# Even chunks, freely issued row-tile blocks and strip maxima on GpSimd in an attention-plus-gate kernel

## The chip, the cores and the metric

The kernel runs on one core of one Trainium2 chip. The metric is device time in microseconds, taken over several executions; one further execution was profiled. A core has TensorE (PE in the profile, its weight loads PEld), VectorE (DVE), ScalarE (ACT), GpSimd (POOL), SyncE (SP), which issues nearly all transfers here, and 16 DMA engines. Each engine runs its own instructions in order and waits on semaphores for the others.

## The reference

```python
# x: [4, 12800, 128], inducing: [32, 128]
def mab(q, kv):
    s = scale * (q @ kv.transpose(0, 2, 1))
    s = s - s.max(-1, keepdims=True)
    a = np.exp(s)
    a /= a.sum(-1, keepdims=True) + 1e-09
    return a @ kv
h = mab(I, x)              # 32 inducing points attend to all tokens of a batch
x = mab(x, h)              # every token attends to the 32 results
...
for k in range(5):         # causal filter of 5 taps along the tokens, per channel
    gate_pre += conv_w[k] * xp[:, k:k + S, :]
gate = 1.0 / (1.0 + np.exp(-gate_pre))
return (gate * (x @ w_val)) @ w_out
```

## The kernel before, in words

Each batch of 12,800 tokens is cut into four strips of 3,200, and the strips into chunks (`SIZES`): in batch 0 eight chunks of 128 to 512 columns, in batches 1 to 3 seven, 480, five times 512, and 160. A chunk always means those columns of all four strips; the strips lie on the four groups of 32 partitions. Two copies of x come from memory: channel-major `xt` (11 buffers) and token-major `xk` (4 buffers); in batch 0 most of `xk` is made on PE from `xt` instead (`make_xk`, letter x).

The first attention goes chunk by chunk. `s1` makes scores with the inducing points (four products side by side, one per strip) and DVE takes them out of PSUM with their maximum. `gmax` combines the maxima of a group of chunks (`GROUPS`) over tokens and strips: a PE product with the identity turns the column of 128 into a row (L420), DVE takes the maximum over strips (L426), small PE products spread it over the partitions again (L434), and DVE scales it (L441). These two halves are the letters gm and gn. `e1` takes exp on ACT and transposes 32x32 blocks on DVE; `h` multiplies with `xk` (L474) and accumulates. `prep` (u) merges the groups and normalises, `prep1` (t) turns the 32x128 result on PE (L532), `prep2` and `prep3` (w, W) scale h by the taps and by w_val and turn that into row-tile weights in two fp16 parts, and `prep_out` (po, pp) finds one scale for the output weights, again over PE (L621, L636).

The second attention, `s2`, makes scores with h (L679), and passes through DVE, POOL, ACT, DVE, POOL, DVE, ACT and POOL to the normalised weights P in two fp16 parts, P1 and P2.

Then come the row-tile blocks (`rblock`). For each chunk and strip, 15 gate units (five taps in three fp16 combinations, L751) and 3 value units (L760) are products with only 32 rows, so the four strips run side by side on the four row tiles of the array. Each chunk has two half blocks. In a half block two strips end their gate units, and the two others do the value units of a chunk and begin the gate units of the next; `SPLIT = 6` gate units stand in the block that begins a gate, nine in the block that ends it, and units are issued row by row over the four strips. After it ACT takes tanh of the gate (L816), DVE multiplies it with the value (L827), ACT and POOL split the product into two fp16 halves (L841, L847), PE multiplies by the output weights (`outp`, L866 to L868), and DVE or ACT evacuates (`evac`, L879 or L881, chosen by `OUTV`), and SP stores.

PE's order is written out by hand: `START` lists everything ahead of the first block, `LEAD` how many half blocks ahead each `s2` stands, `FILL` where the next batch's steps stand between blocks; the two `outp` of a half block follow the next half block. All other engines' orders, SP's included, come from a planner (`Plan.order`): a list schedule with fixed costs, lags and `URGE` offsets, whose due times come from PE's order. The planner makes a fixed program; nothing is decided at run time. Each tile kind has a fixed number of buffers (`BUFS`), and a new user waits for the readers of the buffer that it takes over. Loads also wait for the block `AHEAD` blocks earlier. [...]

Of the kernel before, what the change touches and what calls it, by code (L numbers as in the profile page):

```python
# [29 lines left out]
SIZES = [[128, 256, 512, 512, 512, 512, 512, 256]] + [[480, 512, 512, 512, 512, 512, 160]] * 3  # L30
# [10 lines left out]
SWITCH = 0.09  # L41
# [7 lines left out]
class Plan:  # L49
# [77 lines left out]
    def lay(self, deps, succ, topo, nominal):  # L127
# [8 lines left out]
        free, bus = {}, 1.25  # L136
# [47 lines left out]
def tile_kernel(ctx: ExitStack, tc: tile.TileContext, xt, xk, indT_in, w64, out):  # L184
# [24 lines left out]
    def f_const():  # L209
        warm = const.tile([P, 1], F32, name="warm")  # L210
        V.memset(warm, 0.0)
# [5 lines left out]
        ones = const.tile([P, P], F32, name="ones")  # L217
        V.memset(ones, 1.0)
# [4 lines left out]
        c_.update(ident=ident, identf=identf, ones=ones, pick=pick)  # L223
# [98 lines left out]
    def load_xt(b, c, u=1):  # L322
# [83 lines left out]
    def gmax(b, g):  # L406

        cs = GROUPS[b][g]
        ng = len(GROUPS[b])
# [8 lines left out]
        def f1():
            t = pt(key)
            T.matmul(t[:1, :P], st[m1], c_["identf"], start=True, stop=True)  # L420
# [3 lines left out]
        def f2():
            m = sb(pw, mr, [1, M])
            V.tensor_reduce(m, st[key][:1, :P].rearrange("p (r j) -> p j r", r=R), AX.X, ALU.max)  # L426

        i2 = op("DVE", 0.27, f2, [i1], 0.0, [mr], [key])

        def second():  # L430
            def f4():
                t = pt(key2)
                for r in range(R):
                    T.matmul(t[32 * r:32 * r + 32, :1], st[mr], c_["ones"][:1, :1], start=True, stop=True)  # L434

            i4 = PE(0.17, f4, [i2], [key2], [mr], "strips", 0.12)

            def f5():
                if g == 0:
                    sb(pb, ("ng", b), [P, ng], F32, [P, NCK])  # L440
                V.tensor_scalar(st["ng", b][:, g:g + 1], st[key2][:, :1], -SCALE, None, ALU.mult)  # L441

            ix["ng", b, g] = op("DVE", 0.15, f5, [i4], 0.0, [("ng", b)] * (g == 0), [key2] + [("ng", b)] * (g > 0))

        return second
# [44 lines left out]
    def prep(b):  # L490
# [37 lines left out]
    def prep1(b):  # L528
        key = ("a", "ht", b)

        def f5():
            T.transpose(pt(key)[:, :M], st["hn", b], c_["identf"][:M, :M])  # L532

        i = PE(0.17, f5, [ix["hn", b]], [key], [("hn", b)], lag=0.15)
        ix["hT", b] = op("DVE", 0.18, lambda: V.tensor_copy(sb(pb, ("hT", b), [P, M]), st[key][:, :M]), [i], 0.0,
                         [("hT", b)], [key])

    def prep2(b):
# [77 lines left out]
    def prep_out(b):  # L616

        vmx, wk = ("vmx", b), ("a", "wk", b)

        def f0():  # L620
            T.matmul(pt(wk)[:1, :P], st["q", b], c_["identf"], start=True, stop=True)  # L621

        i0 = PE(0.25, f0, [ix["gsc", b], i_const], [wk], [("q", b)], lag=0.15)

        def f1():
            m = sb(pw, ("qm", b), [1, 1])
            V.tensor_reduce(m, st[wk][:1, :P], AX.X, ALU.max)
            V.tensor_scalar(m, m, TINY, 1.0 / SO, ALU.max, ALU.mult)

        i1 = op("DVE", 0.44, f1, [i0], 0.0, [("qm", b)], [wk])  # L630

        def second():
            key = ("a", "wk2", b)

            def f2():
                T.matmul(pt(key)[:, :1], c_["ones"][:1, :], st["qm", b], start=True, stop=True)  # L636

            i2 = PE(0.2, f2, [i1], [key], [("qm", b)], lag=0.15)

            def f3():  # L640
                V.tensor_scalar(sb(pb, ("osc", b), [P, 1]), st[key][:, :1], 0.5 / SP, None, ALU.mult)
                u = pw.tile([P, 1], F32, name="u")
                V.reciprocal(u, st[key][:, :1])
                V.tensor_scalar(u, u, st[vmx], None, ALU.mult)
                st["u", b] = u

            i = op("DVE", 0.5, f3, [i2], 0.0, [("osc", b)], [key, vmx])
            i = op("ACT", 0.3, lambda: S.activation(sb(pw, ("wof", b), [P, P]), c_["wout"], AF.Copy, scale=st["u", b]), [i],
                   0.0, [("wof", b)])
            i = op("ACT", 0.3, lambda: S.copy(sb(pb, ("wo", b), [P, 2, P], F16)[:, 0], st["wof", b]), [i], 0.0,  # L650
                   [("wo", b)], [("wof", b)])

            def f4():
                G.tensor_tensor(st["wo", b][:, 1], st["wof", b], st["wo", b][:, 0], ALU.subtract)

            ix["wo", b] = op("POOL", 0.42, f4, [i], 0.0, [], [("wof", b), ("wo", b)])

        return second

# [4 lines left out]
    def s2(b, c):  # L664
# [98 lines left out]
    SPLIT = 6  # L763
    seqs = [(b, c) for b in range(B) for c in range(len(SIZES[b]))]

    def rblock(k, half):
# [7 lines left out]
        deps, use, newv, newg = [], [], [], []  # L774
        if cur:
            for r in ends:
                work[r] += [(gate_mm, *cur, r, u) for u in range(SPLIT, len(taps))]
                use.append((f"g{r}", *cur))
        for r in other:
            if val:  # L780
                newv.append(("a", "v", *val, r))
            if nxt:
                newg.append((f"g{r}", *nxt))
            work[r] += [(val_mm, *val, r, u) for u in range(3)] if val else [None] * 3
            work[r] += [(gate_mm, *nxt, r, u) for u in range(SPLIT)] if nxt else []
        for bc in (cur, val, nxt):
            if bc:
                deps += [ix[("P", *bc)], ix["W", bc[0], 1]]
                use += [k for k in (("W", bc[0]),) if k not in use]
        depth = max(len(w) for w in work.values())  # L790

        def part(us, new):
            todo = [[work[r][u] for r in range(R) if u < len(work[r]) and work[r][u]] for u in us]

            def f():
                for row in todo:
                    for fn, *a in row:
                        fn(*a)

            return PE(sum(COST["unit"] * max(SIZES[w[1]][w[2]] for w in row) for row in todo if row) + 0.02,  # L800
                      f, deps, new, use, "rows", 0.34)
# [70 lines left out]
    def evac(b, c, r, i):  # L872
# [57 lines left out]
    def po(b):  # L930
        sec[b, "o"] = prep_out(b)

    def pp(b):
# [139 lines left out]
```

## Time and profile before

| | |
|---|---|
| median of 3 runs | 305.16 us (304.87 to 305.18) |
| profiled execution, its own time | 303.38 us |
| span of the profiled execution, first to last instruction | 301.5 us |
| mean granted clock of PE | 0.984 |
| busy, PE / DVE / ACT / POOL | 286.3 / 236.5 / 216.1 / 204.1 us |
| memory read and written | 48.69 and 26.21 MB |

The page gives busy time per engine, the span in slices, the chain of work that ended last, and groups of instructions by source line with their mean duration. In a timeline row the first number is the start in us, the second the length of the merged piece, and a bracket at the end gives the engine's idle time before it and what ended that. In a row of stretches come the stretch, its length, then busy time and count of PE, PEld, DVE, ACT and POOL, then PE's granted clock (1.00 is full), the DMA engines' mean busy share and GB/s. In a row of groups the numbers are busy us and mean ns, then idle before. A row of waits says who waited for whom: us in total, times, longest.

### The profile page before, as it was taken

To read this page: it belongs to the slowest core of one execution; us is meant where nothing else is said; L and a number is where in the kernel's file an instruction comes from. 1 tells how busy PE (TensorE), PEld (TensorE's weight loads), DVE (VectorE), ACT (ScalarE), POOL (GpSimd) and SP (SyncE) were. 2 spreads that over 40 slices of the span, in tenths; PEclk is the share of its full clock that TensorE was granted. 3 is DMA by queue.
4 is the path that set the end of the run, shared out by engine and by line. 5 is a ranking of instruction groups with operands and counts; after the bars stand their busy time and mean duration, and the time that the engine had idled before them with its cause. 6 is when DMAs were issued, how large, how long until landed. Compare 5 with 4: busy or idle time off the path is not lost.

```text
span 301.5 us, 10231 instructions
## 1 busy us (share of the span) xinstructions
PE 286.3 (95%) x4100; PEld 138.5 (46%) x4100; DVE 236.5 (78%) x597; ACT 216.1 (72%) x421; POOL 204.1 (68%) x229
## 2 busy tenths in 40 slices
PE   7998889999998999999999979999999999999994
PEld 2666435554443346545435324635453444434342
DVE  1568899996695998889668867899788996977562
ACT  2665247587566985887677664789777789889893
POOL 1000457888374798659754494797877999999761
PEclk9999799999999999999999988999999999999998
DMA  7999999698898738979883596922323233244434
GB/s 291 427 407 421 420 417 367 244 404 304 307 357 329 262 127 288 353 273 333 315 296 137 174 361 241 327 95 111 143 104 142 106 133 113 80 157 162 168 141 183
DMA packets 24526, 75.55 MB, mean 251 GB/s; under 512 B 2848, under 2 KB 7456, under 8 KB 19360
## 3 DMA queue, kind: packets, MB, share of 16 engines
q1 hardware_dynamic: 24336, 74.90, 66.0%
q8 instruction: 32, 0.52, 0.7%
q14 instruction: 14, 0.11, 0.1%
q10 hardware_dynamic: 144, 0.02, 0.0%
HBM read 48.69 MB, written 26.21 MB: 248 GB/s over the span
## 4 chain that ended last, share of the span: by engine, by line
PE 69%; DMA 17%; DVE 7%; ACT 3%; issue 2%; SPq 1%; POOL 0%; POOLq 0%; ACTq 0%; DVEq 0%
PE g L751 23%; DMA out_dram<-os 8%; PE a L679 7%; PE a L866 7%; PE a L474 6%; DMA xt<-in_xt_dram 6%; PE a L760 6%; PE a L868 5%; PE a L867 5%; PE a L394 5%; DMA xk<-in_xk_dram 3%; ACT os L881 1%; DVE os L879 1%; PE a L600 1%; DVE tg L827 1%
## 5 line engine op out<-in xcount | busy, mean ns | idle before, releaser
L847 POOL TENSOR_TENSOR gl<-tg,gh 128x512 f16<-128x512 f32 (+4 forms) x112 | 115.4, 1045 | 34.9 <-ACT gh L841 34.2
L751 PE MATMUL g<-P,W 32*128 32x512 f16 (+4 forms) x1740 | 115.0, 345 | 0.2 <-ACT tg L816 0.2
L841 ACT CAST gh<-tg 128x512 f16<-128x512 f32 (+4 forms) x112 | 62.2, 569 | 23.0 <-DVE tg L827 22.5
L827 DVE SCALAR_TENSOR_TENSOR tg<-tg,a 128x512 f32<-128x512 f32 (+4 forms) x116 | 65.7, 604 | 11.8 <-PE a L760 9.5
L751 PEld LDWEIGHTS <-W 32*128 32x128 f16 x1740 | 54.1, 92 | 43.4 <-issue 14.0
L816 ACT ACTIVATE tg<-g,gsc 128x512 f32<-128x512 f32 (+4 forms) x116 | 67.6, 624 | 2.7 <-PE g L751 2.1
L881 ACT ACTIVATE os<-a,osc 128x512 f32<-128x512 f32 (+4 forms) x58 | 36.0, 631 | 15.7 <-PE a L868 9.7
L879 DVE TENSOR_SCALAR os<-a,osc 128x512 f32<-128x512 f32 (+4 forms) x58 | 37.4, 661 | 10.4 <-PE a L868 6.0
L760 PE MATMUL a<-P,W 32*128 32x512 f16 (+4 forms) x348 | 43.7, 348 | 0.7 <-DVE ss L402 0.5
L866 PE MATMUL a<-gh,wo 128*128 128x512 f16 (+4 forms) x112 | 40.0, 359 | 1.4 <-ACT os L881 1.4
L868 PE MATMUL a<-gl,wo 128*128 128x512 f16 (+4 forms) x112 | 39.4, 354 | 0.1
L867 PE MATMUL a<-gh,wo 128*128 128x512 f16 (+4 forms) x112 | 39.4, 354 | 0.0
L737 POOL TENSOR_TENSOR P<-pt,P 128x512 f16<-128x512 f32 (+2 forms) x29 | 30.0, 1037 | 6.4 <-ACT P L730 6.2
L719 POOL TENSOR_TENSOR e<-e,z 128x512 f32<-128x512 f32 (+2 forms) x29 | 27.2, 939 | 8.5 <-DVE z L713 3.3
L394 PE MATMUL a<-xt,indT 128*32 128x512 f32 (+4 forms) x232 | 29.1, 566 | 3.7 <-DMA xt<-in_xt_dram 3.0
L696 POOL TENSOR_TENSOR e<-e,m 128x512 f32<-128x512 f32 (+2 forms) x29 | 27.2, 938 | 5.6 <-DVE m L690 5.1
L474 PE MATMUL a<-xk,et 128*32 128x129 f32 x800 | 28.5, 281 | 1.9 <-DMA xk<-in_xk_dram 0.8
L679 PE MATMUL a<-xt,hT 128*32 128x512 f32 (+2 forms) x232 | 27.4, 556 | 0.0
L474 PEld LDWEIGHTS a<-xk,et 128*32 128x32 f32 x800 | 23.1, 112 | 9.0 <-issue 3.3
L402 DVE TENSOR_SCALAR_CACHE_REDUCE ss<-a 128x512 f32<-128x512 f32 (+4 forms) x29 | 17.5, 606 | 10.9 <-PE a L394 10.2
L702 ACT ACTIVATE e<-e 128x512 f32<-128x512 f32 (+2 forms) x29 | 16.7, 578 | 8.7 <-POOL e L696 8.6
L866 PEld LDWEIGHTS <-wo 128*128 128x128 f16 x112 | 10.8, 97 | 26.4 <-issue 17.6
(104 smaller groups left out, 304.3 us busy)
## 6 DMA issues: line engine op xcount, KB each, us to landing
xt<-in_xt_dram SPq DMA_DIRECT2D x23, 1024.0 KB, 8.7
out_dram<-os SPq DMA_DIRECT2D x80, 256.0 KB, 2.5
xk<-in_xk_dram SPq DMA_DIRECT2D x17, 1032.0 KB, 8.0
xk<-in_xk_dram SPq DMA_DIRECT2D x3, 967.5 KB, 8.8
out_dram<-os SPq DMA_DIRECT2D x12, 240.0 KB, 2.1
xt<-in_xt_dram SPq DMA_DIRECT2D x4, 320.0 KB, 5.5
xt<-in_xt_dram SPq DMA_DIRECT2D x2, 512.0 KB, 8.5
out_dram<-os SPq DMA_DIRECT2D x8, 128.0 KB, 7.5
```

Of the source, the lines that this page charges most:

```text
L394: T.matmul(s[32 * r:32 * r + 32, :n], c_["indT"], x[:, o:o + n // 32, r, :], start=True, stop=True)
L474: T.matmul(t[32 * s:32 * s + 32, :P + 1], e[:, 32 * i:32 * i + 32], x[:, m + i, :], start=i < R, stop=i >= nb - R)
L679: T.matmul(s[32 * r:32 * r + 32, :n], st["hT", b], x[:, m:m + nb, r, :], start=True, stop=True)
L751: T.matmul(st[f"g{r}", b, c][:, :n], st["W", b][q, w, k, :], st[("P1", "P2")[e]][q, o:o + n], start=u == 0, stop=u == len(taps) - 1)
L760: T.matmul(st["a", "v", b, c, r][:, :n], st["W", b][q, w, TAPS, :], st[("P1", "P2")[e]][q, o:o + n], start=u == 0, stop=u == 2)
L816: S.activation(t[:, :n], st[f"g{r}", b, c][:, :n], AF.Tanh, scale=st["gsc", b])
L827: V.scalar_tensor_tensor(t[:, :n], t[:, :n], 1.0, st["a", "v", b, c, r][:, :n], ALU.add, ALU.mult)
L841: S.copy(t, st[tg][:, :n])
L847: G.tensor_tensor(sb(pw, g2, [P, 512], F16)[:, :n], st[tg][:, :n], st[g1][:, :n], ALU.subtract)
L866: T.matmul(t, w[:, 0], st[g1][:, :n], start=True, stop=False)
L867: T.matmul(t, w[:, 1], st[g1][:, :n], start=False, stop=False)
L868: T.matmul(t, w[:, 0], st[g2][:, :n], start=False, stop=True)
```

## The change

- Sizes: batches 1 and 2 get chunks of 448 and 480 columns; batches 0 and 3 keep theirs.
- The number of gate units on each side is chosen per half block by a small dynamic programme over the chunk sizes (`begun`), 6 and 9 in most of batches 1 and 2, up to 8 and down to 1 elsewhere; and within a block each strip's units are put out in the order in which the strips' time is used up, without rows.
- Group maxima over strips and the output scale go from PE to POOL: two maxima of partition halves, then four scalings, one per strip. `gn` and `pp` go away. In batches 1 to 3 h is turned by four 32x32 transposes on DVE.
- In the half blocks listed in `HOLD` the waiting outputs stay until a later block.
- `START`, `FILL`, `LEAD`, `URGE`, `XEV`, `OUTV`, `AHEAD`, batch 0's groups and some of the planner's costs are new; `START` has six groups of filler products (z) on zeros, 11 in all.

```diff
-SIZES = [[128, 256, 512, 512, 512, 512, 512, 256]] + [[480, 512, 512, 512, 512, 512, 160]] * 3
+SIZES = [[128, 256, 512, 512, 512, 512, 512, 256]] + [[448, 448, 448, 448, 448, 480, 480]] * 2 + [[480, 512, 512, 512, 512, 512, 160]]
...
+def begun(n, units, even):
+    last = len(n) - 1
+    ways = {a: (a * n[0] + even * n[0] * (a - 6) ** 2, [a]) for a in range(units + 1)}
+    for k in range(len(n)):
...
+                first = max((units - a) * n[k], (3 * n[k - 1] if k else 0) + b * n[k]) + even * n[k] * (b - 6) ** 2
+                for d in range(units + 1) if k < last else (0,):
+                    second = max((units - b) * n[k], 3 * n[k] + (d * n[k + 1] if k < last else 0))
...
 def gmax(b, g):
-        i1 = PE(0.25, f1, [i0, i_const], [key], [m1], lag=0.2)
...
+            over_strips(st[m1])
+            for r in range(R):
+                G.tensor_scalar(st["ng", b][32 * r:32 * r + 32, g:g + 1], st[m1][:M, 2:], -SCALE, None, ALU.mult)
+        ix["ng", b, g] = op("POOL", 1.3, f1, [i], 0.0, [("ng", b)] * (g == 0), [m1] + [("ng", b)] * (g > 0))
+    def over_strips(m):
+        G.tensor_scalar(m[:2 * M, 1:2], m[:2 * M, :1], m[2 * M:, :1], None, ALU.max)
+        G.tensor_scalar(m[:M, 2:], m[:M, 1:2], m[M:2 * M, 1:2], None, ALU.max)
...
 def prep1(b):
+        def f6():
+            t = sb(pb, ("hT", b), [P, M])
+            for r in range(R):
+                V.transpose(t[32 * r:32 * r + 32], st["hn", b][:, 32 * r:32 * r + 32])
...
 def prep_out(b):
+            V.transpose(t, st["q", b].broadcast_to([P, M]))
+            V.tensor_reduce(sb(pw, qm, [P, 3])[:, :1], t, AX.X, ALU.max)
...
+            over_strips(st[qm])
+            for r in range(R):
+                G.tensor_scalar(u[32 * r:32 * r + 32], st[qm][:M, 2:], TINY, 1.0 / SO, ALU.max, ALU.mult)
+            G.tensor_scalar(sb(pb, ("osc", b), [P, 1]), u, 0.5 / SP, None, ALU.mult)
...
 def rblock(k, half):
+            while any(work.values()) and (whole or any(w and w[0][0] is val_mm for w in work.values())):
+                r = min((r for r in range(R) if work[r]), key=lambda r: (spent[r], r))
+                fn, b, c, r, u = work[r].pop(0)
+                todo.append((fn, b, c, r, u))
+                spent[r] += COST["unit"] * SIZES[b][c]
...
-            for o in late:
-                outp(*o)
-            late = [(*seqs[q], r) for r in rs] if 0 <= q < len(seqs) else []
+            if 2 * k + half not in HOLD:
+                for o in late:
+                    outp(*o)
+                late = []
+            late += [(*seqs[q], r) for r in rs] if 0 <= q < len(seqs) else []
...
-OUTV = [(2, 3), (0, 2), (0, 1), (0, 2)]
-AHEAD = 18
+OUTV = [(0,), (2,), (2, 3), (2,)]
+AHEAD = 11
+TURNED = (0,)
+EVEN = 0.02
+HOLD = (0, 5, 7, 9, 13, 16, 19, 24, 28, 31, 38, 40, 43)
```

In batch 0 the new START makes `xk` of chunks 0, 2, 3, 1, 5 and 6 on PE (before: 0, 2, 1, 3, 5 and 7) and loads 4 and 7 (before: 4 and 6). Ahead of the first block it also holds `s1` of chunk 3 and the products `h` of chunks 0 and 2 of batch 1; before, those came later, and `s1` of chunks 0, 1 and 2 were there in both.

More of the change, by code (lines that the diff above doesn't have):

```diff
@@ L1 @@
+import functools
 import itertools
@@ L40 @@
 OWN = 0.035
-SWITCH = 0.09
+SWITCH = dict(full=0.09, rows=0.095, strips=0.117)
 COST = dict(
@@ L88, in order @@
             deps[b].append(a)
-            ops[a]["turn"] = SWITCH * (ops[a]["kind"] != ops[b]["kind"])
+            ops[a]["turn"] = SWITCH[ops[a]["kind"]] * (ops[a]["kind"] != ops[b]["kind"])
         succ = [[] for _ in range(n)]
@@ L135, in lay @@
                 late[i] = min(late[i], late[s] - ops[i]["dur"] - ops[i]["lag"])
-        free, bus = {}, 1.25
+        free, bus = {}, 1.45
         end = [0.0] * n
@@ L175, in lay @@
         return seq, at, end
+@functools.lru_cache(None)
+def begun(n, units, even):
+    last = len(n) - 1
+    ways = {a: (a * n[0] + even * n[0] * (a - 6) ** 2, [a]) for a in range(units + 1)}
+    for k in range(len(n)):
+        more = {}
+        for a, (c, way) in ways.items():
+            for b in range(units + 1):
+                first = max((units - a) * n[k], (3 * n[k - 1] if k else 0) + b * n[k]) + even * n[k] * (b - 6) ** 2
+                for d in range(units + 1) if k < last else (0,):
+                    second = max((units - b) * n[k], 3 * n[k] + (d * n[k + 1] if k < last else 0))
+                    v = c + first + second + (even * n[k] * (d - 6) ** 2 if k < last else 0)
+                    if d not in more or v < more[d][0]:
+                        more[d] = v, way + [b, d]
+        ways = more
+    return min(ways.values())[1]
 def cost(kind, n):
@@ L216, in f_const @@
         make_identity(nc, identf)
-        ones = const.tile([P, P], F32, name="ones")
-        V.memset(ones, 1.0)
         pick = const.tile([P, M], F32, name="pick")
@@ L222, in f_const @@
             st[k] = const.tile([P, XW], F16, name=k)
-        c_.update(ident=ident, identf=identf, ones=ones, pick=pick)
+        c_.update(ident=ident, identf=identf, pick=pick)
     def f_ind():
@@ L332, in f @@
             nc.sync.dma_start(st[key][:, first:first + n // 32].rearrange("p i r q -> p (i r q)"), xt[b, :, o:o + R * n])
-        ix["xt", b, c, u] = sp(n * 2048 / BW + 1.9 * ((b, c) == (0, 2)), f, [key] * own, [key] * (not own))
+        ix["xt", b, c, u] = sp(n * 2048 / BW + 1.2 * ((b, c) == (0, 2) and ("xt", 0, 1, 1) in ix), f, [key] * own, [key] * (not own))
     def load_xk(b, c):
@@ L409, in gmax @@
         ng = len(GROUPS[b])
-        key, key2 = ("a", "gm", b, g), ("a", "gn", b, g)
-        m1, mr = ("m1", b, g), ("mr", b, g)
+        m1 = ("m1", b, g)
         def f0():
-            V.tensor_reduce(sb(pw, m1, [P, 1]), st["mx", b][:, cs[0]:cs[-1] + 1], AX.X, ALU.max)
-        i0 = op("DVE", 0.15, f0, [ix["ss", b, c] for c in cs], 0.0, [m1], [("mx", b)])
+            V.tensor_reduce(sb(pw, m1, [P, 3])[:, :1], st["mx", b][:, cs[0]:cs[-1] + 1], AX.X, ALU.max)
+        i = op("DVE", 0.15, f0, [ix["ss", b, c] for c in cs], 0.0, [m1], [("mx", b)])
         def f1():
-            t = pt(key)
-            T.matmul(t[:1, :P], st[m1], c_["identf"], start=True, stop=True)
-        i1 = PE(0.25, f1, [i0, i_const], [key], [m1], lag=0.2)
[L424 to L445, printed above, removed]
+            if g == 0:
+                sb(pb, ("ng", b), [P, ng], F32, [P, NCK])
+            over_strips(st[m1])
[5 more added lines that the diff above has]
+        G.tensor_scalar(m[:M, 2:], m[:M, 1:2], m[M:2 * M, 1:2], None, ALU.max)
     def e1(b, g, c):
@@ L501, in prep @@
         i0 = op("DVE", 0.15, f0, [ix["ng", b, g] for g in gs] + [i_const], 0.0, [f_], [("ng", b)])
-        i0 = op("ACT", 0.2, lambda: S.activation(st[f_], st["ng", b], AF.Exp, bias=st["mt", b], scale=-1.0), [i0], 0.0, [],
+        i0 = op("ACT", 0.29, lambda: S.activation(st[f_], st["ng", b], AF.Exp, bias=st["mt", b], scale=-1.0), [i0], 0.0, [],
                 [f_, ("ng", b)])
@@ L508, in f1 @@
                 S.activation(sb(pw, Ds[g], [P, M]), c_["pick"], AF.Copy, scale=st[f_][:, g:g + 1])
-        i0 = op("ACT", 0.13 + 0.16 * len(gs), f1, [i0], 0.0, Ds, [f_])
+        i0 = op("ACT", 0.1 + 0.215 * len(gs), f1, [i0], 0.0, Ds, [f_])
         Hs = [("H", b, g) for g in gs]
@@ L529, in prep1, with f5 @@
         key = ("a", "ht", b)
[L531 to L536, printed above, removed]
+        if b in TURNED:
+            def f5():
+                T.transpose(pt(key)[:, :M], st["hn", b], c_["identf"][:M, :M])
+            i = PE(0.17, f5, [ix["hn", b]], [key], [("hn", b)], lag=0.15)
+            ix["hT", b] = op("DVE", 0.18, lambda: V.tensor_copy(sb(pb, ("hT", b), [P, M]), st[key][:, :M]), [i], 0.0,
+                             [("hT", b)], [key])
+            return
+        def f6():
+            t = sb(pb, ("hT", b), [P, M])
+            for r in range(R):
+                V.transpose(t[32 * r:32 * r + 32], st["hn", b][:, 32 * r:32 * r + 32])
+        ix["hT", b] = op("DVE", 0.84, f6, [ix["hn", b]], 0.0, [("hT", b)], [("hn", b)])
     def prep2(b):
@@ L561, in g1 @@
                             st[cg][:, :, None].broadcast_to([P, TAPS, M]), ALU.mult)
-        ig = op("POOL", 0.65, g1, [i], 0.0, [wf, cg], [("hT", b)])
+        ig = op("POOL", 0.81, g1, [i], 0.0, [wf, cg], [("hT", b)])
         ih = op("ACT", 0.325, lambda: S.copy(sb(pw, w2, [P, 2, TAPS + 1, M], F16)[:, 0, :TAPS], st[wf]), [ig], 0.0,
@@ L616, in prep_out @@
     def prep_out(b):
-        vmx, wk = ("vmx", b), ("a", "wk", b)
+        vmx, tq, qm = ("vmx", b), ("tq", b), ("qm", b)
         def f0():
-            T.matmul(pt(wk)[:1, :P], st["q", b], c_["identf"], start=True, stop=True)
-        i0 = PE(0.25, f0, [ix["gsc", b], i_const], [wk], [("q", b)], lag=0.15)
+            t = sb(pw, tq, [P, M])
+            V.transpose(t, st["q", b].broadcast_to([P, M]))
+            V.tensor_reduce(sb(pw, qm, [P, 3])[:, :1], t, AX.X, ALU.max)
+        i = op("DVE", 0.4, f0, [ix["gsc", b]], 0.0, [tq, qm], [("q", b)])
@@ L625, in f1 @@
         def f1():
[L626 to L656, printed above, removed]
@@ L658, in prep_out, with f2 @@
-        return second
+            u = st["u", b] = pw.tile([P, 1], F32, name="u")
+            over_strips(st[qm])
+            for r in range(R):
+                G.tensor_scalar(u[32 * r:32 * r + 32], st[qm][:M, 2:], TINY, 1.0 / SO, ALU.max, ALU.mult)
+            G.tensor_scalar(sb(pb, ("osc", b), [P, 1]), u, 0.5 / SP, None, ALU.mult)
+        i = op("POOL", 1.5, f1, [i], 0.0, [("osc", b)], [qm])
+        def f2():
+            u = st["u", b]
+            V.reciprocal(u, u)
+            V.tensor_scalar(u, u, st[vmx], None, ALU.mult)
@@ new lines, in prep_out, with f4 @@
+        i = op("DVE", 0.38, f2, [i], 0.0, [], [vmx])
+        i = op("ACT", 0.35, lambda: S.activation(sb(pw, ("wof", b), [P, P]), c_["wout"], AF.Copy, scale=st["u", b]), [i],
+               0.0, [("wof", b)])
+        i = op("ACT", 0.32, lambda: S.copy(sb(pb, ("wo", b), [P, 2, P], F16)[:, 0], st["wof", b]), [i], 0.0,
+               [("wo", b)], [("wof", b)])
+        def f4():
+            G.tensor_tensor(st["wo", b][:, 1], st["wof", b], st["wo", b][:, 0], ALU.subtract)
+        ix["wo", b] = op("POOL", 0.42, f4, [i], 0.0, [], [("wof", b), ("wo", b)])
@@ L713, in sm @@
                 V.memset(z[:M, 0, :1], 0.0)
-        i = op("DVE", cost("dve", n) + 0.52, sm, [i], 0.0, [zk], [ek])
+        i = op("DVE", cost("dve", n) + 0.55, sm, [i], 0.0, [zk], [ek])
         def nm():
@@ L761, in val_mm @@
                  start=u == 0, stop=u == 2)
-    SPLIT = 6
     seqs = [(b, c) for b in range(B) for c in range(len(SIZES[b]))]
+    split = begun(tuple(SIZES[b][c] for b, c in seqs), len(taps), EVEN)
     def rblock(k, half):
@@ L773, in rblock @@
         work = {r: [] for r in range(R)}
-        deps, use, newv, newg = [], [], [], []
         if cur:
             for r in ends:
-                work[r] += [(gate_mm, *cur, r, u) for u in range(SPLIT, len(taps))]
-                use.append((f"g{r}", *cur))
+                work[r] += [(gate_mm, *cur, r, u) for u in range(split[2 * k + half], len(taps))]
         for r in other:
[L780 to L785, printed above, removed]
+            work[r] += [(val_mm, *val, r, u) for u in range(3)] if val else []
@@ L786, in rblock @@
+            work[r] += [(gate_mm, *nxt, r, u) for u in range(split[2 * k + half + 1])] if nxt else []
+        deps, held = [], []
         for bc in (cur, val, nxt):
-            if bc:
+            if bc and any(w[1:3] == bc for l in work.values() for w in l):
                 deps += [ix[("P", *bc)], ix["W", bc[0], 1]]
[L789 to L793, printed above, removed]
-            def f():
[L796 to L801, printed above, removed]
@@ L803, in rblock, with part @@
-        i0 = part(range(3), newv)
-        i = part(range(3, depth), newg)
+                held += [k for k in (("W", bc[0]),) if k not in held]
+        spent = {r: 0.0 for r in range(R)}
+        def part(whole):
+            todo, new, use, before = [], [], list(held), max(spent.values())
+            while any(work.values()) and (whole or any(w and w[0][0] is val_mm for w in work.values())):
[3 more added lines that the diff above has]
+                spent[r] += COST["unit"] * SIZES[b][c]
+                key = ("a", "v", b, c, r) if fn is val_mm else (f"g{r}", b, c)
+                if u == 0:
+                    new.append(key)
+                elif key not in new and key not in use:
+                    use.append(key)
+            def f():
+                for fn, *a in todo:
+                    fn(*a)
+            return PE(max(spent.values()) - before + 0.02, f, deps, new, use, "rows", 0.34)
@@ L805, in rblock @@
+        i0 = part(False) if val else None
+        i = part(True)
         blocks.append(i)
@@ L883, in evac @@
         v = r in OUTV[b]
-        j = op("DVE" if v else "ACT", cost("psum", n) if v else cost("act", n) + 0.06, ev, [i], 0.0, [os], [key, ("osc", b)])
+        j = op("DVE" if v else "ACT", cost("psum", n) + 0.07 if v else cost("act", n) + 0.06, ev, [i], 0.0, [os], [key, ("osc", b)])
         def store():
@@ L940, in xs @@
         make_xk(b, c, XEV[c])
-    do = dict(s1=S1, z=idle, gm=gm, gn=gn, h=hh, x=xs, u=prep, t=prep1, w=prep2, k=load_xk,
-              W=prep3, po=po, pp=pp, s2=s2, l=lambda b, c: ("xt", b, c, 1) in ix or load_xt(b, c))
+    do = dict(s1=S1, z=idle, gm=gmax, h=hh, x=xs, u=prep, t=prep1, w=prep2, k=load_xk,
+              W=prep3, po=prep_out, s2=s2, l=lambda b, c: ("xt", b, c, 1) in ix or load_xt(b, c))
     for b, f, *a in START:
@@ L1023 @@
 WARM = 8
-LEAD = [[10.5, 0, 11.5, 6.5, 2.5, 13, 6.5, 6.5], [2, 2, 3, 9.5, 3.5, 4, 7.5], [1.5, 3, 2, 6, 3.5, 6, 5.5], [3.5, 4, 6, 6.5, 8, 6, 5]]
-AHEAD = 18
+LEAD = [[-9.5, 13, 0.5, 8, 4.5, 13, 4, 6], [2, 4.5, 4.5, 3, 5, 5.5, 14], [1.5, 2, 3.5, 7.5, 4.5, 3.5, 11.5], [3, 7.5, 2.5, 7.5, 11, 8.5, 2.5]]
+AHEAD = 11
 AGAIN = [(), (), (), ()]
-BUFS = dict(xt=11, wf=2, cg=2, hn=2, wof=1, xk=4, ss=4, et=3, e=3, pt=2, tg=5, gh=4, gl=4, q=2, qm=2, osc=2, os=4, H=4, mx=2, ng=2, m1=2, mr=2, f=2, D=6, hT=2,
+BUFS = dict(xt=11, wf=2, cg=2, hn=2, wof=1, xk=4, ss=4, et=3, e=3, pt=2, tg=5, gh=4, gl=4, q=2, qm=2, tq=2, osc=2, os=4, H=4, mx=2, ng=2, m1=2, f=2, D=6, hT=2,
             gmx=2, vmx=2, gsc=2, wo=2, w2=2, W=2, m2=3, z=3, a=4, g0=1, g1=1, g2=1, g3=1)
```

17 lines of the change are left out of this document (4 added, 13 removed), and 37 rows, old and new, of tables (FILL, START).

## The prediction

> **What bounds the kernel now.** I read the page's engine rows, slices and chain first, then a table of stretches, then the tensor engine's own waits.
>
> ```profile
> span 301.5 us, 10231 instructions
> PE 286.3 (95%) x4100; PEld 138.5 (46%) x4100; DVE 236.5 (78%) x597; ACT 216.1 (72%) x421; POOL 204.1 (68%) x229
> PE 69%; DMA 17%; DVE 7%; ACT 3%; issue 2%; SPq 1%; POOL 0%; POOLq 0%; ACTq 0%; DVEq 0%
> ...
> 30.00:40.00 10.00, 8.91 (x124) 4.60 (x127) 8.79 (x39) 2.21 (x5) 3.81 (x8) 0.83 1.01 421
> ...
> 90.00:100.00 10.00, 8.55 (x104) 3.38 (x103) 6.64 (x15) 6.28 (x11) 4.53 (x5) 1.00 0.88 330
> ...
> 160.00:180.00 20.00, 17.65 (x278) 7.50 (x272) 16.52 (x36) 15.40 (x27) 13.05 (x14) 0.98 0.63 221
> ...
> 240.00:260.00 20.00, 19.82 (x286) 9.09 (x282) 16.83 (x39) 18.09 (x39) 19.59 (x22) 1.00 0.29 106
> 260.00:280.00 20.00, 20.00 (x246) 7.96 (x236) 15.87 (x31) 18.64 (x34) 19.50 (x20) 1.00 0.41 156
> ```
>
> PE is busy 95% of the span and carries 69% of the chain; no other engine passes 78%. After about 60 us nearly every stretch has PE at 20.0 of 20 us, so the time there is the sum of what PE is given to do, plus a few waits. Before that, the opening mixes loads and latency. Two cautions: POOL is at 98% from 240 to 280 us (19.59 and 19.50 of 20) and ACT at 90 to 93%, so helpers have little room late.
>
> ```profile
> PE a L866 <- ACT os L881: 1.4, 1, 1.4
> ...
> 179.37 1.94 PE L394 MATMUL a<-xt,indT 128*32 128x512 f32 x8 [2.00 <-DMA xt<-in_xt_dram]
> 33.00:34.00 1.00, 1.00 (x33) 0.79 (x32) 0.96 (x4) 0.25 (x1) 0.67 (x2) 0.50 1.05 429
> 180.00:181.00 1.00, 1.00 (x8) 0.25 (x4) 0.00 (x0) 0.00 (x0) 1.00 (x1) 0.50 0.98 355
> ```
>
> Later waits are few: 2.0 us for one x tile at 179 us, 1.4 us for one evacuation, some tenths elsewhere. Twice the granted clock is halved (0.50 in the last two rows). The first time it makes the 0.83 of the stretch 30 to 40 us: 0.17 of 10 us, 1.7 us lost; I take the same for the second.
>
> **The change, part by part.** The sum is made against the profiled span of 301.5 us. That execution took 303.38 us, 1.88 us more than its span; the median of the runs shown, 305.16 us, is 0.6% above it. I add my difference to the median.
>
> *Row-tile blocks.* A block runs two lists of 32-row matmuls, two tiles each, concurrently, and lasts as long as the longer list. Before, gate units were split 9 and 6 everywhere and the four tiles went row by row, so where a 512-column chunk is followed by one of 160 the lists are 9x512 = 4608 against 3x512+6x160 = 2496 columns, and one pair of tiles idles. Summing the longest list over all 60 blocks from SIZES gives 243,648 columns before. With the new chunks, the chosen splits and each tile going on freely, the same sum is 235,104; perfectly even would be 230,400. The difference is 8,544 columns. The price:
>
> ```profile
> 269.67 0.39 PE L751 MATMUL g<-P,W 32*128 32x512 f16 x2
> ...
> 271.73 0.39 PE L866 MATMUL a<-gh,wo 128*128 128x512 f16 x1
> ...
> 169.81 1.06 PE L679 MATMUL a<-xt,hT 128*32 128x512 f32 x8
> 170.81 0.39 PE L760 MATMUL a<-P,W 32*128 32x512 f16 x2
> ...
> 87.45 1.06 PE L679 MATMUL a<-xt,hT 128*32 128x512 f32 x8
> 88.33 1.04 PE L394 MATMUL a<-xt,indT 128*32 128x512 f32 x8
> ```
>
> A score product takes 1.00 us start to start when a block follows (169.81 to 170.81) and 0.88 when another score product does (87.45 to 88.33): a change between full, strip and row shapes costs 0.12 us. A block of nine 512-column steps takes 271.73-269.67 = 2.06 us, less 0.12 is 1.94, or 0.215 us for 512 columns. So 8,544 columns are **-3.6 us**, nearly all after 60 us, where PE has no other bound.
>
> *Matmuls that leave PE.* The group maximum (L420, then L434), the output scale (L621, L636) and the turned h (L532) leave PE, the last in three batches of four.
>
> ```profile
> 195.80 1.06 PE L679 MATMUL a<-xt,hT 128*32 128x512 f32 x8
> 196.68 0.38 PE L420 MATMUL a<-identf,m 128*1 128x128 f32 x2
> 196.99 0.39 PE L751 MATMUL g<-P,W 32*128 32x512 f16 x2
> ...
> 200.04 0.24 PE L434 MATMUL a<-ones,mr 1*32 1x1 f32 x8
> 200.21 0.38 PE L866 MATMUL a<-gh,wo 128*128 128x480 f16 x1
> ...
> 185.84 0.38 PE L621 MATMUL a<-identf,q 128*1 128x128 f32 x2
> 186.15 0.39 PE L866 MATMUL a<-gh,wo 128*128 128x512 f16 x1
> 191.88 0.38 PE L636 MATMUL a<-qm,ones 1*128 1x1 f32 x2
> 192.12 0.45 PE L760 MATMUL a<-P,W 32*128 32x480 f16 x2
> ...
> 218.22 0.19 PE L532 MATMUL a<-identf,hn 32*128 32x32 f32 x1
> 218.34 0.39 PE L866 MATMUL a<-gh,wo 128*128 128x512 f16 x1
> ```
>
> Start to start they cost 0.31 (less 0.12 for the shape change that stays: 0.19), 0.17, 0.31, 0.24 and 0.12 us. Six group maxima and three of each other kind lie in batches 1 to 3: 6x0.36 + 3x0.55 + 3x0.12 = 4.2 us. Batch 0's share, 3x0.36 + 0.55 = 1.6 us, lies in the opening, where PE partly waits anyway; I take half. **-5.0 us** (bounds -4.2 and -5.8).
>
> *Shape changes.* Writing out PE's order from START, FILL, LEAD and HOLD, without those matmuls, gives 146 changes of shape from block (2,1) on before and 134 after: where HOLD lets outputs wait, four follow in one go. 12 x 0.12 = **-1.4 us**. In the opening it is 31 and 29, which I count as nothing: PE waits there in any case, and would cost 0.2 us without that cover.
>
> *What PE gets in addition.* Chunk 6 instead of chunk 7 is transposed on PE, 76 transposes for 68.
>
> ```profile
> 20.07 1.97 PE L370 MATMUL g<-identf,xt 128*128 128x128 f32 x16
> 21.97 0.27 PE L420 MATMUL a<-identf,m 128*1 128x128 f32 x1
> 26.25 2.70 PE L474 MATMUL a<-xk,et 128*32 128x129 f32 x77 [0.81 <-DMA xk<-in_xk_dram]
> L895 PE MATMUL a<-zero 128*128 128x512 f16 x8 | 3.6, 631 | 1.2 <-DVE warm L211 1.2
> ```
>
> Sixteen take 1.90 us, so eight more are 0.95, and a fourth group in batch 0 about 0.1: **+1.05 us**. Eleven filler matmuls (z) stand in the opening, at most 3.6/8 = 0.45 us each, 5.0 us together, at the cold rate, and half of that at full clock, 2.5. Most stand where PE waited (the 0.81 us above is one such wait; the stretch 30 to 40 us has 1.09 us idle). I take **+0.5**, bounds 0 and +2.5. They fill the sparse time ahead of the first half-clock stretch; avoiding it would bring 1.7 us, not avoiding it nothing: **-0.8**. [...]
>
> *Loads.* Chunk 4's token-major tile was the fifth in a pool of four, so it waited for a product and PE then for it, 0.81 us; now it is the fourth: **-0.8**. x tiles still reuse 11 buffers. Adding up PE's order at the prices above, the wait at 179 us came where the product that frees the buffer stands 6.6 us of work ahead of its next user; the closest such pairs after 60 us are then 7.7 and 8.5 us apart.
>
> ```profile
> DMA to landing us min/median/max: 5.4/6.8/8.2
> ```
>
> With landings of 5.4 to 8.2 us there, that wait may shrink but isn't gone. AHEAD 11 for 18 lets loads start later, but eleven blocks are at least 11 x 2.06 = 23 us, and a landing is 8.2: nothing.
>
> *What the other engines get.* Rows that set the prices:
>
> ```profile
> L559 POOL TENSOR_SCALAR cg<-w,gs 128x5 f32<-128x5 f32 x4 | 1.1, 273 | 9.6 <-DVE vmx L571 8.5 <-DVE gs L553 1.0
> L881 ACT ACTIVATE os<-a,osc 128x512 f32<-128x512 f32 (+4 forms) x58 | 36.0, 631 | 15.7 <-PE a L868 9.7
> L881 ACT ACTIVATE os<-a,osc 128x160 f32<-128x160 f32 x6 | 2.4, 398 | 1.8 <-DMA out_dram<-os 1.1 <-PE a L858 0.6
> ```
>
> POOL gets 10 group maxima of six small operations and 4 output scales of seven, 88 at no more than the 0.27 us of a small operation: up to 24 us, from 204 to at most 228 of about 292 us. OUTV moves 22 evacuations from DVE to ACT, 22 x 0.63 = 14 us: ACT 230. DVE falls by about as much, less the 32x32 transposes it gains. None becomes the busiest; I cost this at nothing because PE's fixed order covers it. Without that cover each group maximum could hold back a product and everything behind it. The end does change: three of the last four 160-column evacuations are now on ACT, one more at 0.4 us, of which **+0.3** shows.
>
> *The remaining waits* after 60 us (1.45, 2.35 and 0.18 us idle in three stretches of the table, 4.0 together, and 1.7 us of half clock) I leave as they are: a new order removes some and makes others. Bounds: -6 if all go; +8 if they more than double, from the 98% POOL and the 93% ACT above.
>
> Sum: -3.6 -5.0 -1.4 +1.05 +0.5 -0.8 -0.8 +0.3 = -9.75 us: span 291.8, the median 295.4 us.
>
> **The rivals.** *Savings become waits.* PE asks for each result 3% sooner from helpers that are 90 to 98% busy late; for it speak the 98% POOL, against it that PE waits for none of them from 260 to 280 us (20.0 of 20). At 4 to 9 us given back: 299 to 304.5 us.
>
> *The waits go as well.* The second half clock (1.7), the 2.0 and the 1.4 us and most of the tenths go, 5 to 7 us more: 288.5 to 290.5 us.
>
> *Slower, by the group maximum on GpSimd.* Six dependent small operations stand in POOL's queue behind operations of over 1 us, then exp, transpose and the product that PE has at a fixed place. Chain: 0.68 (maximum per chunk) + 6x0.27 + 0.72 (exp) + 0.70 (transpose) = 3.7 us after the last score product.
>
> ```profile
> L402 DVE TENSOR_SCALAR_CACHE_REDUCE ss<-a 128x512 f32<-128x512 f32 x20 | 13.5, 680 | 5.6 <-PE a L394 5.2
> L453 ACT ACTIVATE ss<-ss,ng 128x512 f32<-128x512 f32 x20 | 13.7, 716 | 3.1 <-DVE ng L441 3.1
> L458 DVE STREAM_TRANSPOSE et<-ss 128x512 f32<-128x512 f32 x20 | 13.8, 697 | 0.8 <-ACT ss L453 0.8
> ```
>
> The shortest room, counted the same way, is some 4.5 us (batch 1, first group) and 6 to 7 in batch 3. It decides against the change from 1 us lost at each of ten groups, which takes queues of 3 us or more: 306 to 309 us. [...]
>
> *The change doesn't do what it says:* if the tiles don't run on freely, the first term shrinks, to about -2.5 us (the new chunks alone, counted in the old manner): 296.5, inside the forecast's range.
>
> **How the numbers follow.** Forecast (291 to 298.5 us) 0.57; savings become waits 0.20; waits go as well 0.13; slower 0.07; within 0.2%, about what a measurement can tell (304.5 to 305.8), 0.03. So 295.4 us; the range, leaving out some of the two outer cases, 289.5 to 302. Faster 0.90, same 0.03, slower 0.07.
>
> **What would show it.** Right: PE stays above 94% busy in a span near 292; L420's, L434's and L621's kind of matmul are gone from PE; block rows pass a batch's end without the half-empty 512-to-160 step; the stretch 30 to 40 us has a clock above 0.83; POOL's small operations add no more than 24 us and PE's wait list stays under 6 us after 60 us. Wrong: PE waits of several us at the products of exp (L474) released by POOL's maxima, ACT at 20 of 20 in batch 3 with PE idle, or new 0.50 clock stretches.

## Result and the profile after

The changed kernel takes 294.19 us (292.06 to 294.54, four runs), the kernel before 305.17 us beside it: a ratio of 0.963 (0.958 to 0.967). Forecast were 295.4 us, range 289.5 to 302. The profiled execution took 294.48 us. Medians are of all executions, and ratios leave out slow ones (beside e5 to e8 one of 13 of the kernel before: 306.13 us at a granted clock of 0.983, where the median is 302.12), so the two can differ by a microsecond. From the page of the changed kernel: span, busy time, granted clock in slices, and the chain of work that ended last.

```profile
span 292.7 us, 10189 instructions
PE 278.4 (95%) x4012; PEld 135.7 (46%) x4012; DVE 225.0 (77%) x567; ACT 222.8 (76%) x441; POOL 223.3 (76%) x317
...
PEclk9999999999999999999799999999999999999999
...
PE 65%; POOL 11%; DMA 7%; DVE 5%; ACT 5%; issue 4%; POOLq 0%; SPq 0%; ACTq 0%; DVEq 0%
```

PE's busy time falls by 7.9 us and the span by 8.8, so PE is still 95% busy. (Busy time also grew where the clock was halved: by the stretches at 0.50, about 3.4 us of the 286.3 before and 1.7 of the 278.4 are that; the executions of e12 and e9 below, with whole clock, have 282.9 and 277.0.) POOL was not on the chain before and has 11% of it now. Stretches of the changed kernel:

```profile
30.00:40.00 10.00, 8.74 (x131) 3.83 (x121) 8.45 (x38) 1.43 (x4) 4.50 (x17) 1.00 1.02 419
...
90.00:100.00 10.00, 9.99 (x134) 3.80 (x122) 9.52 (x26) 8.64 (x17) 8.62 (x15) 1.00 0.77 280
...
120.00:140.00 20.00, 17.86 (x280) 9.09 (x278) 15.44 (x37) 17.02 (x37) 14.89 (x21) 0.98 0.88 327
140.00:160.00 20.00, 20.00 (x310) 10.33 (x307) 13.70 (x40) 14.58 (x29) 13.49 (x20) 0.94 0.95 346
...
240.00:260.00 20.00, 19.39 (x219) 8.31 (x218) 14.43 (x26) 17.98 (x33) 19.86 (x21) 1.00 0.38 144
260.00:280.00 20.00, 20.00 (x258) 7.91 (x256) 11.76 (x24) 19.23 (x36) 16.76 (x17) 1.00 0.37 139
```

The clock is whole from 30 to 40 us (0.83 before), the 1.45 us idle at 90 to 100 us are gone, and a new stall stands at 120 to 140 us (2.14 us idle), with a half-clock stretch behind it (0.94 of the next 20 us).

To see where the time came from I use two marks that both programs have: the first output product of batch 0's second chunk, and the last product of all. Timelines of PE, first the kernel before, then the changed one:

```profile
57.71 0.28 PE L866 MATMUL a<-gh,wo 128*128 128x256 f16 x1
...
295.89 1.62 PE L858 MATMUL a<-tg,wof 128*128 128x160 f32 x8
```

```profile
32.80 0.21 PE L536 MATMUL a<-identf,hn 32*128 32x32 f32 x1 [0.98 <-DVE hn L527]
...
60.02 0.28 PE L873 MATMUL a<-gh,wo 128*128 128x256 f16 x1
...
286.82 1.60 PE L865 MATMUL a<-tg,wof 128*128 128x160 f32 x8
```

The opening takes 2.3 us more (60.02 for 57.71), the middle 226.8 us for 238.2, 11.4 less, and the tail 5.9 for 5.6. PE's steps ahead of the first mark differ little: one score product of batch 1 more (`s1`) and one of `s2` fewer. So all of the gain is in the middle.

### The profile page after: what moved, and what is told of

Same layout as the page of the kernel before. It is cut to its first block, busy times and chain, and to the rows that moved or that the text cites. A ratio compares the mean times of both kernels' runs of the same rounds, so it can differ in the third digit from the quotient of the medians.

```text
span 292.7 us, 10189 instructions
## 1 busy us (share of the span) xinstructions
PE 278.4 (95%) x4012; PEld 135.7 (46%) x4012; DVE 225.0 (77%) x567; ACT 222.8 (76%) x441; POOL 223.3 (76%) x317
## 4 chain that ended last, share of the span: by engine, by line
PE 65%; POOL 11%; DMA 7%; DVE 5%; ACT 5%; issue 4%; POOLq 0%; SPq 0%; ACTq 0%; DVEq 0%
PE g L754 20%; PE a L477 8%; PE a L873 6%; PE a L682 6%; PE a L763 6%; PE a L875 5%; PE a L874 5%; PE a L413 5%; POOL gl L854 4%; DMA out_dram<-os 4%; DMA xt<-in_xt_dram 3%; POOL P L740 2%; POOL ng L441 2%; ACT os L888 1%; ACT ss L456 1%
## 5 line engine op out<-in xcount | busy, mean ns | idle before, releaser
L754 PE MATMUL g<-P,W 32*128 32x512 f16 (+5 forms) x1740 | 110.6, 345 | 0.3 <-ACT tg L823 0.3
L834 DVE SCALAR_TENSOR_TENSOR tg<-tg,a 128x512 f32<-128x512 f32 (+5 forms) x116 | 65.7, 604 | 21.2 <-PE a L763 16.7
L823 ACT ACTIVATE tg<-g,gsc 128x512 f32<-128x512 f32 (+5 forms) x116 | 66.7, 627 | 12.5 <-PE g L754 10.2
L754 PEld LDWEIGHTS <-W 32*128 32x128 f16 x1740 | 52.1, 92 | 43.8 <-issue 15.2
L888 ACT ACTIVATE os<-a,osc 128x512 f32<-128x512 f32 (+5 forms) x80 | 48.2, 632 | 6.6 <-DMA out_dram<-os 3.8
L763 PE MATMUL a<-P,W 32*128 32x512 f16 (+5 forms) x348 | 43.9, 348 | 0.8 <-DVE os L886 0.6
L740 POOL TENSOR_TENSOR P<-pt,P 128x512 f16<-128x512 f32 (+4 forms) x29 | 29.8, 1032 | 4.1 <-ACT P L733 4.0
L413 PE MATMUL a<-xt,indT 128*32 128x512 f32 (+5 forms) x232 | 27.8, 545 | 2.6 <-DMA xt<-in_xt_dram 1.7
L699 POOL TENSOR_TENSOR e<-e,m 128x512 f32<-128x512 f32 (+4 forms) x29 | 27.1, 936 | 2.8 <-DVE m L693 1.6
L722 POOL TENSOR_TENSOR e<-e,z 128x512 f32<-128x512 f32 (+4 forms) x29 | 27.1, 936 | 2.5 <-DVE z L716 1.8
L682 PE MATMUL a<-xt,hT 128*32 128x512 f32 (+4 forms) x232 | 25.8, 545 | 0.1
```

The lines of the kernel that those rows point to most:

```text
L682: T.matmul(s[32 * r:32 * r + 32, :n], st["hT", b], x[:, m:m + nb, r, :], start=True, stop=True)
L754: T.matmul(st[f"g{r}", b, c][:, :n], st["W", b][q, w, k, :], st[("P1", "P2")[e]][q, o:o + n], start=u == 0, stop=u == len(taps) - 1)
L763: T.matmul(st["a", "v", b, c, r][:, :n], st["W", b][q, w, TAPS, :], st[("P1", "P2")[e]][q, o:o + n], start=u == 0, stop=u == 2)
L823: S.activation(t[:, :n], st[f"g{r}", b, c][:, :n], AF.Tanh, scale=st["gsc", b])
L834: V.scalar_tensor_tensor(t[:, :n], t[:, :n], 1.0, st["a", "v", b, c, r][:, :n], ALU.add, ALU.mult)
L888: S.activation(o, a, AF.Copy, scale=st["osc", b])
```

## The experiments

Each run stands beside the kernel before on its own chip, where that kernel took about 302 us rather than 305; so I compare medians taken on the same chip, or ratios. Beside e1 to e4 the changed kernel did not run again; its 294.2 us there is that of the first result.

**e5: the changed kernel again.**

> The changed kernel unchanged, beside the following three on one chip. By the sum of steps it stands 9 to 11 us below the kernel before on any chip. If part of the difference was made by stretches of half clock that only some executions have: 7 us or less where the kernel before runs without its second one.

294.01 us against 302.12: 8.1 us by the medians, ratio 0.972 (0.964 to 0.980), which is 8.4 us. That lies between the two expectations. So the difference was 11 us in the first result and 8 here. The changed kernel took 294 us both times; why the kernel before took 305 us once and 302 later is not shown.

**e1: the old blocks in the new order** (`SIZES` and `rblock` of before, `SPLIT = 6`).

> The changed kernel with the chunk sizes, the 9 and 6 split and the row-by-row issue of the kernel before; all else stays. If the sum of PE's work sets the time: 8,544 columns more at 0.215 us per 512, +3.6 us on 294.2, so 297.8 us. If block rows only fill time in which PE would wait: within 1 us of 294.2.

302.36 us, 1.003 of the kernel before: about 8 us are lost, more than twice the 3.6 expected. PE's busy time rises by 4.5 us (282.9 for 278.4), or 5.9 over e9 below, whose clock is whole (277.0). Its rows (L754 and L763) take 161.6 us where the changed kernel's take 154.5, and where the same old blocks in the old order take 158.7: in this order the old blocks also lose time inside the rows, which the profile counts as busy. The rest are waits, of which this row shows the largest:

```profile
243.03 0.38 PE L871 MATMUL a<-gl,wo 128*128 128x512 f16 x1 [1.71 <-POOL gl L850]
```

**e7: the new blocks in the old order** (`SIZES`, `begun` and `rblock` of the change put into the kernel before).

> The kernel before with the new chunk sizes, the chosen splits and the freely issued blocks, its order of all other steps kept. If PE's work sets the time: 8,544 columns fewer, 3.6 us less. If the order decides, which was made for the old sizes: between 3 us less and 3 us more.

302.35 us, ratio 0.998 (0.993 to 1.003): no difference. PE's busy time, first row, falls from 286.3 to 282.9 us, which looks like the 3.6 us of the columns, but isn't. About 1.7 us of it is the half clock behind the 179 us wait, which this execution didn't have. The old blocks in the old order have 282.9 us as well when the clock is whole (second row, from e12 below). The rows (L772 and L781 here) take 157.4 us where L751 and L760 took 158.7, or 158.2 in e12: in the old order about 1 us of the columns' 3.6 shows.

```profile
PE 282.9 (95%) x4100; PEld 137.6 (46%) x4100; DVE 236.4 (79%) x597; ACT 214.6 (72%) x421; POOL 203.8 (68%) x229
...
PE 282.9 (95%) x4100; PEld 136.0 (46%) x4100; DVE 236.9 (80%) x597; ACT 216.4 (73%) x421; POOL 204.0 (69%) x229
```

**e6: maxima on GpSimd in the old order** (`gmax`, `prep_out` of the change; gn and pp struck from the lists).

> The kernel before with group maxima and output scale on GpSimd, its order of all other steps kept. If PE's work sets the time: 4.2 us less (0.36 us for each of six group maxima, 0.55 for each of three scales, 0.4 for the opening's share, and shape changes), up to 5.4. Rival, POOL's queue: the six operations delay gl and P, and half or more comes back as waits: 0 to 2 us less.

308.09 us, 1.018 (1.009 to 1.028): slower by 5 to 6 us, which neither expectation had. PE waits 5.2 us at two x tiles where the kernel before waits 2.0 us at one, more than half of the loss:

```profile
182.09 1.07 PE L394 MATMUL a<-xt,indT 128*32 128x512 f32 x8 [3.17 <-DMA xt<-in_xt_dram]
196.96 1.38 PE L394 MATMUL a<-xt,indT 128*32 128x512 f32 x8 [2.04 <-DMA xt<-in_xt_dram]
```

The loads of these two tiles are issued later than in the kernel before (173.12 us for 171.06, 187.06 for 186.00) and take longer to land (8.8 and 9.8 us for 8.2 and 8.1). Why was not followed.

**e2: maxima on PE again in the new order**, in two steps each, with places like those of before.

> The changed kernel with group maxima and output scale on PE again (gm, gn, po, pp, at places near those of the new order). If PE's work sets the time: +4.2 to +5.4 us (0.36 us for each of ten groups, 0.55 for each of four scales, less what hides in the opening), 298.4 to 299.6 us. If instead the maxima on GpSimd only exchange PE time for POOL time and latency: 293 to 295 us, since POOL gets 20 us back.

320.23 us, far beyond both expectations. The run says little about PE's price: I probably put the second steps too close ahead of the products that need them, and its wait list has exp's chain at its head:

```profile
PE a L495 <- DVE et L479: 9.1, 6, 2.4
```

**e3: no output held back.**

```diff
-HOLD = (0, 5, 7, 9, 13, 16, 19, 24, 28, 31, 38, 40, 43)
+HOLD = ()
```

> The changed kernel with no output held back (HOLD empty). By PE's work: 178 changes of shape for 167, 11 x 0.12 = +1.3 us, 295.5 us. Rival: the four outputs in a row cause the wait of 2.1 us at 138 us (an evacuation waits for its store) and the 1.7 us of half clock after it; then both go and the time is about 291.7 us.

298.20 us, ratio 0.989 (0.985 to 0.992), some 4 us worse than the changed kernel. The rival is refuted: without four outputs in a row evacuations still wait for stores, 4.7 us in all (3.8 in the changed kernel).

```profile
ACT os L888 <- DMA out_dram<-os: 4.7, 3, 2.0
```

**e4: no filler products.**

> The changed kernel without its 11 filler products in the opening. If they stand only where PE would wait and keep the clock up: no gain, and a half-clock stretch between 30 and 40 us comes back, 294.2 to 296 us. If they cost their own time: 11 x 0.22 = 2.4 us less, 291.8 us, with the clock at 1.00.

294.46 us, beside 294.0 to 294.2 with them: no difference, and the first output product of the second chunk comes at 60.20 us for 60.02. The clock is whole, and waits take the fillers' places in the opening. The last row is from the stall that the changed kernel has at 138 us:

```profile
PEclk9999999999999999999999999999999999999999
...
27.50 2.77 PE L477 MATMUL a<-xk,et 128*32 128x129 f32 x80 [1.21 <-DVE et L461]
41.06 1.95 PE L477 MATMUL a<-xk,et 128*32 128x129 f32 x56 [1.52 <-issue]
...
140.59 1.07 PE L477 MATMUL a<-xk,et 128*32 128x129 f32 x28 [3.11 <-ACT os L888]
```

So the fillers are not what keeps the clock whole. Nor is the old order of the opening what halves it: e7 and e12 both have PE's old order there and no fillers, and the clock of 30 to 40 us is 0.83 in e7 (first row) and 1.00 in e12:

```profile
30.00:40.00 10.00, 9.19 (x131) 4.96 (x132) 8.70 (x40) 2.20 (x5) 3.79 (x8) 0.83 1.02 420
...
30.00:40.00 10.00, 8.73 (x133) 3.63 (x134) 8.98 (x42) 2.20 (x5) 3.80 (x8) 1.00 1.02 425
```

What decides it stays open. The length of the idle alone doesn't: PE stood still for 3.11 us in e4, longer than the 2.14 us of the changed kernel, and the clock stayed whole.

**e8 and e9: six store buffers** (`os=6` for `os=4`).

> The changed kernel with six buffers for evacuated outputs instead of four. If the wait of 2.1 us at 138 us comes from an evacuation that waits for the store of its buffer: it goes, with the half clock behind it, 2 to 4 us less than the changed kernel. If the wait is ACT's load, nothing changes: within 0.5 us of the changed kernel.

> The changed kernel with six store buffers once more, as the base of the next two on the same chip: 0.955 to 0.970 of the kernel before.

290.46 us, 3.6 below the changed kernel on the same chip by the medians and 2.6 by the ratios, and 290.72 in e9; ratios 0.963 (0.958 to 0.969) and 0.962 (0.958 to 0.966). This is the fastest version here. The chain of the changed kernel around the stall, SP's timeline ahead of it, and PE's clock behind it:

```profile
127.44 10.51 DMA out_dram<-os
...
138.04 0.64 ACT os L888
...
138.73 1.43 PE a L477 x25
```

```profile
122.00 0.94 SPq L362 DMA_DIRECT2D xk<-in_xk_dram  x2
...
124.99 1.12 SPq L351 DMA_DIRECT2D xt<-in_xt_dram  x2
127.44 12.15 SPq L894 DMA_DIRECT2D out_dram<-os  x6
```

```profile
139.00:140.00 1.00, 1.00 (x28) 0.90 (x16) 0.00 (x0) 1.00 (x3) 0.24 (x1) 0.53 0.49 192
140.00:141.00 1.00, 1.00 (x6) 0.28 (x3) 0.29 (x1) 1.00 (x3) 1.00 (x2) 0.50 1.34 379
```

Four loads of about 1 MB are issued from 122 to 126 us, and the store issued after them takes 10.5 us to land; that the loads are what holds it up is a reading, not tested. Its buffer is the one that the next evacuation needs; ACT waits, its PSUM buffer stays taken, PE waits 2.14 us, and in this execution then runs at half clock. With six buffers the wait list has only this left of it:

```profile
PE a L477 <- ACT os L888: 0.2, 1, 0.2
```

**e12: six store buffers in the kernel before.**

> The kernel before with six store buffers. If stores hold back evacuations there as well: its waits of 1.45 us at 94 us and some tenths go, 1 to 3 us less than before. If four were enough there, since no four outputs follow in a row: within 0.6 us of it.

298.59 us against 302.03, ratio 0.989 (0.983 to 0.996): about what the first expectation had. ACT's waits for stores (L881), 5.4 us in all before, are gone, and with them PE's 1.4 us at L866, so here too stores held evacuations back. With six buffers on both sides the change is worth 7.9 us (290.72 against 298.59).

**e10: the removed PE steps added back as idle products** on constants, with nobody waiting for them, in the version with six buffers.

```diff
+        def f():
+            T.matmul(pt(key)[:1, :P], c_["identf"][:, :1], c_["identf"], start=True, stop=True)
+        PE(0.25, f, [i_const], [key])
```

> Six store buffers, and PE also runs the 28 small matmul steps of the old group maxima and output scales, on constants and with nobody waiting for the result; the maxima themselves stay on GpSimd. If the removed matmuls cost PE their start-to-start time: 3.5 us (those after the block that starts near 60 us) to 5.8 us above the base. If what the old maxima cost was only their latency and their waits: within 1 us of the base.

302.20 us, 11.5 above its base, where 3.5 to 5.8 were expected. (There are 28 steps, for ten groups and four scales; the kernel before had nine groups, so 26.) Start to start the step shown costs what the prediction took, and yet new waits stand elsewhere:

```profile
220.11 0.38 PE L935 MATMUL a<-identf 128*1 128x128 f32 x2
220.42 0.36 PE L873 MATMUL a<-gh,wo 128*128 128x448 f16 x1
...
242.90 0.36 PE L875 MATMUL a<-gl,wo 128*128 128x480 f16 x1 [1.70 <-POOL gl L854]
```

0.31 us from the step to the next product, as in the kernel before. PE is busy 7.3 us more (284.3 for 277.0). Each step also takes one of the four general PSUM buffers in turn, and the planner makes new orders for the other engines; which of these made the waits was not separated.

**e11: old blocks with six store buffers.**

> Six store buffers, with chunk sizes, split and row-by-row issue of the kernel before. If the 8 us lost by the same edit with four buffers were 3.6 us of columns and the rest waits for stores: 3 to 5 us above the base. If the old blocks break an order that was made for the new ones: 6 to 9 us above it, with waits on several engines.

300.40 us, 9.7 above the base: nearest to the second expectation, and beyond its 9 us. Waits for stores were not what made e1 lose so much.

## Why the prediction was right, step by step

The total came out at 295.4 for 294.2 us, but with two errors of opposite sign, so that its closeness is in part luck. Against the span, to which the terms were added, 9.75 us less were forecast and 8.8 measured.

*Opening.* Its terms summed to -0.85 us (-0.8 small steps, +1.05, +0.5 and -0.8 for fillers and clock, -0.8 load); measured is +2.3. The failing step is counting PE's work where PE waits for a latency chain. The product that turns h starts at 32.80 us where it started at 30.84, which is 2.0 of the 2.3 us: an x tile is waited for 1.42 us at 8.93 us (the longest such wait there was 0.62 us), transposes and a score product of the next batch now stand ahead of it, and it waits 0.98 us for DVE. The wait for chunk 4's tile did go, without profit. Fillers are worth nothing either way (e4), so +0.5 misses; the clock was whole here, but not by the fillers, and e12 has it whole without the change, so the -0.8 can't be put down to the change. That the fillers would keep it whole was my estimate, and no run shows it; nor does a long idle stand ahead of the clock of 0.50 near 33 us in the kernel before, where PE had waited at most 0.81 us at a time from 2 us on.

*Middle.* Rows -3.6, small steps -4.2 and shape changes -1.4 are -9.2 us; measured is -11.4. The waits that I left as they were fell: from about 4.9 us of marked PE waits after 60 us to 3.2. The tile wait at 179 us is gone and the store wait at 138 us is new, each with 1.7 us of half clock behind it in these executions; the evacuation's 1.4 us is gone too. The new half-clock stretch is one of the signs that the prediction named as wrong; it came, and did not decide the time.

*Rows.* PE's busy time on L754 and L763 is 154.5 us, where L751 and L760 had 158.7: -4.2 for the -3.6 forecast, or -3.7 against e12's 158.2, which has no half clock.

*Small steps.* The prices hold start to start (e10). As a cause of time, they and the rows are not additive: e1 and e11 lose 8 to 10 us for 3.6, e10 loses 11.5 for 5.8, and in the old order the same two parts bring nothing (e7) or a loss (e6). PE 95% busy made the sum good for the whole, by my reading because the new order keeps PE supplied; it didn't make each term a price for its part alone. No run has the new order with neither part, and in every run the planner also makes new orders for the other engines, so what the order is worth by itself stays open.

*Shape changes.* e3 has the sign and three times the size.

*Tail.* 5.88 for 5.61 us: the +0.3 of one more evacuation on ACT.

*Other engines.* POOL rose by 19.2 us, within the bound of 24. Groups of its new operations:

```profile
L441 POOL TENSOR_SCALAR ng<-m 32x1 f32<-32x1 f32 x40 | 8.4, 209 | 2.8
L448 POOL TENSOR_SCALAR m<-m 32x1 f32<-32x1 f32 x10 | 2.9, 291 | 1.0
L447 POOL TENSOR_SCALAR m<-m 64x1 f32<-64x1 f32 x10 | 2.8, 285 | 14.2 <-DVE m L432 13.5
```

A maximum takes 0.29 us, a scaling 0.21: 2 x 0.29 + 4 x 0.21 = 1.4 us for a group. The idle before each operation is about 0.1 us where DVE's maximum is not awaited (2.8 us for the 40 scalings, 1.0 for the ten maxima of the second row).

PE never waits directly for these operations in the changed kernel, but once it does through exp. Timelines of POOL, ACT and PE at the first group of batch 1, the one whose room the prediction found shortest:

```profile
37.81 0.28 POOL L447 TENSOR_SCALAR m<-m 64x1 f32<-64x1 f32 x1
...
39.59 1.23 ACT L456 ACTIVATE ss<-ss,ng 128x448 f32<-128x448 f32 x2 [1.06 <-POOL ng L441]
...
41.04 1.27 PE L477 MATMUL a<-xk,et 128*32 128x129 f32 x28 [1.32 <-issue]
```

DVE had the group's maximum ready at 36.76 us, but POOL was still busy with the output scale and one operation more, and began 1.05 us later; exp waited for the scalings, and PE for exp's transpose, which ended at 40.94 us. So the slower rival's chain came about at one group of ten, in the opening, at about 1.3 us: too little to decide. In the old order (e6), more than half of the time lost was lost at loads.

## What to carry to other kernels

With PE 95% busy, the sum of its work forecast the whole here (295.4 for 294.2 us), but not what each part brings under another order (the rows 8 us in e1, nothing in e7): test parts in both orders before believing a price. An opening bound by latency wants its chain added up, not the busy engine's work (-0.85 us forecast, +2.3 measured). Compare busy time between executions with the same clock: PE's 4,100 products of the kernel before took 286.3 us with two stretches at 0.50 and 282.9 in e12 without. When an evacuation waits on a store, look at which loads were issued just ahead of it (10.5 us to land behind four loads); two more buffers were worth about 3 us in both kernels (3.6 in e8, 3.4 in e12).

## What was not expected of the hardware

A 224 KB store, issued after about 4 MB of loads, took 10.5 us to land, where the median of the 40 of its size is 2.1 us. The clock went to half for about 3.4 us after 2.14 us of idle PE, but not after 3.11 us at the same place in e4; and with the same order of PE it was halved near 33 us in one execution (kernel before, 0.50) and whole in another (e12, 1.00).
